# A planned mixer kernel: class statistics moved to ScalarE, the first tile in halves, and an order chosen among drawn ones

## The chip, the cores and the metric

The kernel runs on one core of a Trainium2 chip. The core has five engines that run at the same time and each take their own instructions in order: TensorE (PE: matrix products; PEld are its weight loads), VectorE (DVE), ScalarE (ACT), GpSimd (POOL) and SyncE (SP), which here issues transfers (DMA). The metric is the device time of one launch in microseconds (us), the median of several runs.

## What is computed

A sliding, dilated attention and a channel MLP, both on the same normalised input, multiplied and added to it (32 heads of 16, window 8, dilation 2, 2048 rows of 512, MLP width 1376):

```python
xn = _layernorm(x)
# A: q, k, v from xn @ wqkv; row s attends to rows s, s-2, ..., s-14
logits = einsum("bhsd,bhswd->bhsw", q, kg) * scale      # masked with -1e9 where s-2w < 0
attn = softmax(logits)
s = einsum("bhsw,bhswd->bhsd", attn, vg).reshape(B, S, D) @ wo
# B: normalised again, then Dense-GELU-Dense
y = _layernorm(xn)
g = silu(gelu(y @ w1 + b1) @ w2 + b2)
return x + s * g
```

## The kernel before

**Data.** Even and odd rows never meet in the attention, so there are two classes `c` of 1024 rows, each in eight tiles of 128 rows (`NI = 8`). Float32 values enter products as a high and a low float16 half, so that a product takes three matmuls (high·high, high·low, low·high); weights are scaled by powers of two found from their sums of squares.

**Start.** The tiles of class 0 are loaded and normalised in the order 2, 3, 0, 1, (4, 5), (6, 7) (`GROUPS`, `ln0`, L550). Per group: VectorE takes mean and variance (`stats`, L533); POOL works out the scaling (`factors`, L503: two small linear steps on the variance at L514 and L524, powers of −1/2 at L517 and L526, products at L521, L528 and L530); VectorE scales the tile (L571), or ScalarE for groups in `ACT_Y` (`y_act`, L538); TensorE transposes it (L578); ScalarE copies the result (L584, for tiles 2 and 3, which TensorE then multiplies in float32 at L651 while the weights are still being split) or casts it to its high half (L590), and VectorE takes the low half (L592). Until there is real work, TensorE runs `WAKE0` + `WAKE` idle matmuls (L1063).

**Weights.** `prep_q` (L469) finds the scale of a block of wqkv and splits it (L474, L492, L494). The MLP's w1 is squared and summed by ScalarE in four pieces (L392); the high halves of all four are written by VectorE (L443, `W1DVE`), the low halves too (L446). w2 follows (L445, L446).

**Units.** There are eight units `u`, a class and a block of eight heads each. `qkv` (L623) makes q, k and v of a unit in one of two buffers U (L644, ScalarE evicts at L661; halo copies by DMA at L670). `attention` (L689) then works on VectorE: four products q·k (L704), each summed over the 16 columns of a head (L707), maximum, difference (L727, L728), exponential on ScalarE (L730), sum, reciprocal, scaling (L732 to L734), four products with v (L760) that are added up (L755), a part of that by POOL "beside" VectorE (L783, L784), output halves (L743, L745) and a transposing DMA (L748). A buffer U is free for `qkv` of unit u + 2 once the unit's products have been taken.

**MLP.** `mlp1` (L905) multiplies one of 11 blocks of w1 with 512 rows (L914), Gelu at L931, high half at L935; the low half is made by VectorE (L939) where the step's number is in `DVE_LO`, else by a product on TensorE that subtracts the high half (L945) and ScalarE (L948). `mlp2` (L952, product at L961) follows two steps behind; Silu at L977. Results of the first product lie in two buffers `mh`.

**Class 1.** `ln1` (L597) loads each of the eight tiles, takes mean and variance by `stats` on VectorE, then `factors` for all eight, loads them again, scales them on ScalarE (L539), and makes the halves (L613, L614), which a transposing DMA brings into place (L616). **End.** `wo_first` and `wo_last` multiply with wo (L830), multiply with the MLP's result, and `finish` (L819) adds x: on VectorE for all tiles of class 0 (L821), on POOL for every second tile of class 1 (L823).

**Order.** Nothing is issued while the kernel is described: `Plan.add` notes each operation with its engine, a duration, what it reads and writes, and a priority. `Plan.issue` (L204) then places all of them on a modelled clock: per engine it takes, of those that could start soonest, the one with the lowest priority number, gives it buffers, and moves the clock; the instructions are then emitted in the order found. `port=True` marks VectorE and POOL operations that the model doesn't let overlap; ScalarE operations with a `table` that is not loaded cost 1.3 more. So a change of one constant can move any instruction.

Of the kernel before, what the change touches and what calls it, by code (L numbers as in the profile page):

```python
# [38 lines left out]
GROUPS = [(2,), (3,), (0,), (1,), (4, 5), (6, 7)]  # L39
# [4 lines left out]
ACT_Y = (1, 4, 5)  # L44

W1DVE = (0, 1, 2, 3)
# [7 lines left out]
DVE_LO = range(8, 44)  # L54
# [23 lines left out]
class Op:  # L78
    __slots__ = ("eng", "dur", "fn", "prio", "table", "bufs", "preds", "succs", "npred",
                 "ready", "nbytes", "n", "port", "rate", "issue", "tail", "slack")  # L80


class Plan:
# [9 lines left out]
    def add(self, eng, dur, fn, reads=(), writes=(), prio=None, table=None, nbytes=0,  # L93
            after=None, holds=(), port=False, rate=350e3, issue=0.55, tail=1.4, slack=0.0):
# [16 lines left out]
        o.port, o.rate, o.issue, o.tail, o.slack = port, rate, issue, tail, slack  # L111
        o.prio = self.prio if prio is None else prio
# [39 lines left out]
    def start(self):  # L152
        for o in self.ops:
            o.npred, o.ready, o.succs = len(o.preds), 0.0, []
        for o in self.ops:
            for p in o.preds:
                p.succs.append(o)
        self.free = {o.eng: 0.0 for o in self.ops}
        self.portfree, self.dma, self.landed, self.table = 0.0, 0.0, [], None

# [8 lines left out]
    def place(self, o, t):  # L169
# [15 lines left out]
        if o.eng == "act" and o.table is not None and o.table != self.table:  # L185
            end += 1.3
            self.table = o.table
        self.free[o.eng] = end
        if o.port:
            self.portfree = end  # L190
# [13 lines left out]
    def issue(self):  # L204
# [6 lines left out]
        while len(order) < len(self.ops):  # L211
            best = None
            for e, cand in engs.items():
                lst = []
                for o in cand:
                    t = self.earliest(o)
                    ok = True
# [18 lines left out]
            engs[o.eng].remove(o)  # L236
            for b in o.bufs:
                if b.slot is None:
                    r = b.ring.free
                    b.slot = r.index(min(r))  # L240
                    r[b.slot] = float("inf")
# [6 lines left out]
            for x in self.done(o, end, MARGIN):  # L248
                engs[x.eng].append(x)
            order.append((t, o))  # L250
        self.end = max(self.free.values())
        for t, o in order:
            o.fn()

# [16 lines left out]
WAKE0 = 26  # L271
# [28 lines left out]
def tile_mixer(ctx, tc, a_x, a_wqkv, a_wo, b_w1, b_b1, b_w2, out):  # L300
# [18 lines left out]
    def dve(n, fn, r, w, f=1.0, port=True, c=0.065, **k):  # L319
        pl.add("dve", c + n * DVE1 * f, fn, r, w, port=port, **k)  # L320

    def act(n, fn, r, w, aps=1, **k):
        pl.add("act", 0.07 + n * ACT1 + 0.093 * aps, fn, r, w, **k)
# [113 lines left out]
    def split(hi, lo, src, s, r, w, eng="act", n=None):  # L437
# [6 lines left out]
        else:  # L444
            act(n, lambda: nc.scalar.activation(hi, get(), AF.Identity, scale=s), r, [(w, "hi")])  # L445
        dve(n, lambda: nc.vector.scalar_tensor_tensor(lo, get(), s, hi, op0=ALU.mult,  # L446
                                                      op1=ALU.subtract), r + [(w, "hi")], [w], c=0.125)
# [21 lines left out]
    def prep_q(hb):  # L469
        col = R_s.new()  # L470
        for k in range(0, KT, 2):
# [5 lines left out]
            act(768, go, [("stq", hb, k)] + ([("yf", 2)] if hb == 0 else []), [(col, k), ("wqh", hb, k), ("wqh", hb, k + 1)],  # L477
# [8 lines left out]
        for k in range(0, KT, st):  # L486
# [9 lines left out]
                r + hk, [("wq", hb, j) for j in range(k, k + st)], holds=stkey[hb], c=0.125,  # L496
# [6 lines left out]
    def factors(n, mv, mk, cdst, ckeys, bias=True, pp=None):  # L503
# [6 lines left out]
        V = lambda: mv()[:, 0:n, 1]  # L510
        a0 = lambda: A.t[:, 0:n]
        a1 = lambda: A.t[:, 8:8 + n]
        small, power = 0.21, 0.42 + 0.14 * n
        pool(small, lambda: nc.gpsimd.tensor_scalar(  # L514
            p0b.t[:, 0:n], V(), (1.0 + EPS) / YS ** 2, EPS * EPS / YS ** 2, op0=ALU.mult, op1=ALU.add),
            mk, [p0b], prio=pp, port=False)
        pool(power, lambda: nc.gpsimd.tensor_tensor(  # L517
            rb.t[:, 0:n], p0b.t[:, 0:n], halves[:, 0:n], op=ALU.pow), [p0b], [(rb, 0)], prio=pp, port=False)
        if bias:
            for a in range(n):  # L520
                pool(small, lambda a=a: nc.gpsimd.tensor_scalar(  # L521
                    rb.t[:, 8 + a:9 + a], mv()[:, a:a + 1, 0], rb.t[:, a:a + 1], -1.0, op0=ALU.mult, op1=ALU.mult),
                    [mk[a], (rb, 0)], [(rb, 1, a)], prio=pp, port=False)
        pool(small, lambda: nc.gpsimd.tensor_scalar(  # L524
            a0(), V(), EPS, YS ** -2, op0=ALU.add, op1=ALU.mult), mk, [(A, 0)], port=False)
# [731 lines left out]
```

## Time and profile before

The page reports busy time per engine (an engine is busy while an instruction runs on it), the stretches in which it idled, and what ended a wait; "L661" is a line of the kernel, "ps<-wq,yT" its output and inputs.

| | |
|---|---|
| median of 3 runs | 422.49 us (421.89 to 422.58) |
| the profiled execution, its time | 421.77 us |
| the profiled execution, its span | 420.0 us |
| L914, L961: first and second MLP product, main forms | 456 and 480 matmuls of 512 columns, a group of 12 takes 2.59 us |
| L644: q, k, v | 744 matmuls of 384 columns, 12 take 1.95 us |
| L704, L707 on VectorE | 32 × 2290 ns, 32 × 2280 ns |
| L760, L755 on VectorE, 2048 columns | 28 × 2285 ns, 16 × 2282 ns |
| L535, L536: mean and variance | 16 × 0.68 us, 16 × 0.18 us |
| L784 on POOL | 21 × 2.35 us |
| L931, L935 on ScalarE, main forms | 38 × 749 ns, 38 × 684 ns |
| ScalarE table loads | 1283 ns each, 8 of them at L730 |

A group of matmuls advances TensorE by less than the sum of their durations, as they overlap. A busy share close to one on two engines says that either can hold the other; which of them does is read from the waits of each stage.

### The profile page before, as it was taken

Reading aid. Unit: us, or ns where it says so; the run is one execution under the profiler, and the core shown is the slowest. Engines: PE = TensorE matmul, PEld = TensorE weight load, DVE = VectorE, ACT = ScalarE, POOL = GpSimd, SP = SyncE. Lnnn points to the kernel's source line nnn. Section 1 sums busy time; section 2 is a strip of 40 time slices with the busy share of each in tenths; the row PEclk is TensorE's granted clock in tenths of the full one; section 3 lists DMA queues with packets and bytes.
Section 4 is the critical chain, followed back from the end, with each engine's and each line's share of the span. In section 5 each row is a group of like instructions: output and inputs, shape, how many; then the busy total and the mean of one; then the engine's idle time right before and its main releaser. Section 6 shows DMA issues by size and latency. Waiting matters only on the chain.

```text
span 420.0 us, 5549 instructions
## 1 busy us (share of the span) xinstructions
PE 410.1 (98%) x2107; PEld 209.5 (50%) x2107; DVE 387.7 (92%) x365; ACT 211.6 (50%) x314; POOL 91.8 (22%) x166
## 2 busy tenths in 40 slices
PE   7989999999999999999999999999999999999995
PEld 5556544445554465445544654454445544444442
DVE  4867999999999999899999999999999989999983
ACT  3899983953437842853358335334121393236400
POOL 7810200000463043002500430052002500250031
PEclk9999999999999999999999999999999999999999
DMA  8964440120025247611262022006423383007152
GB/s 298 413 234 140 126 163 0 61 91 0 2 87 126 77 108 163 154 39 26 87 151 100 2 87 52 1 20 193 150 85 123 88 209 111 2 0 204 52 144 102
DMA packets 42666, 44.83 MB, mean 107 GB/s; under 512 B 27496, under 2 KB 27936, under 8 KB 42128
## 3 DMA queue, kind: packets, MB, share of 16 engines
q1 hardware_dynamic: 42640, 44.49, 35.0%
q8 instruction: 16, 0.26, 0.3%
q14 instruction: 10, 0.08, 0.1%
HBM read 23.53 MB, written 7.34 MB: 74 GB/s over the span
## 4 chain that ended last, share of the span: by engine, by line
PE 78%; DVE 10%; POOL 3%; issue 3%; DMA 2%; ACT 1%; SPq 0%; DVEq 0%; POOLq 0%; ACTq 0%
PE ps L644 22%; PE z L961 22%; PE mh L914 21%; PE ps L830 6%; PE z L830 2%; DVE prod L704 2%; PE mh L644 2%; DVE prod L760 2%; DVE L L707 2%; PE mh L830 1%; PE ps L914 1%; DMA U<-U 1%; DVE f L614 1%; POOL lw L517 1%; DMA f<-in_A_x_dram 1%
## 5 line engine op out<-in xcount | busy, mean ns | idle before, releaser
L914 PE MATMUL mh<-yT,w 128*128 128x512 f16 (+1 forms) x504 | 115.5, 379 | 0.1
L644 PE MATMUL ps<-wq,yT 128*128 128x384 f16 x684 | 114.5, 326 | 0.9 <-ACT U L661 0.8
L961 PE MATMUL z<-w,h 128*128 128x512 f16 x480 | 111.4, 379 | 0.6 <-ACT f L977 0.6
L644 PEld LDWEIGHTS <-yT 128*128 128x128 f16 x744 | 72.7, 98 | 49.5 <-issue 1.1
L914 PEld LDWEIGHTS <-w 128*128 128x128 f16 (+1 forms) x528 | 52.8, 100 | 61.3 <-issue 0.4
L961 PEld LDWEIGHTS <-h 128*128 128x128 f16 x480 | 47.0, 98 | 56.0 <-issue 1.1
L704 DVE TENSOR_TENSOR prod<-U 128x2048 f32<-128x2048 f32 x32 | 73.1, 2290 | 1.6 <-DMA U<-U 0.6
L707 DVE TENSOR_REDUCE L<-prod 128x128 f32<-128x2048 f32 x32 | 72.8, 2280 | 0.4
L931 ACT ACTIVATE mh<-mh,b1T,hsc 128x512 f32<-128x512 f32 (+1 forms) x42 | 31.4, 749 | 81.5 <-PE mh L914 81.4
L760 DVE TENSOR_TENSOR prod<-L,U 128x2048 f32<-128x2048 f32 x28 | 63.5, 2285 | 0.3
L661 ACT ACTIVATE U<-ps,cs 128x384 f32<-128x384 f32 x58 | 33.0, 578 | 56.1 <-PE ps L644 50.0
L783 POOL COPY gate<-prod 1x1 f32<-1x1 f32 x21 | 4.4, 208 | 238.3 <-DVE prod L704 235.0
L755 DVE TENSOR_TENSOR prod<-prod,prod 128x2048 f32<-128x2048 f32 x16 | 36.5, 2282 | 0.0
L784 POOL TENSOR_TENSOR prod<-prod 128x1024 f32<-128x1024 f32 x14 | 32.9, 2349 | 0.0
L830 PEld LDWEIGHTS <-oT 128*128 128x128 f16 x189 | 18.5, 98 | 22.1
L830 PE MATMUL ps<-wo,oT 128*128 128x512 f16 x120 | 27.2, 379 | 0.0
L935 ACT ACTIVATE h<-mh,hsc 128x512 f16<-128x512 f32 x38 | 26.0, 684 | 0.8
L939 DVE SCALAR_TENSOR_TENSOR h<-mh,hsc,h 128x512 f16<-128x512 f32 x32 | 23.9, 746 | 2.1 <-ACT h L935 2.0
L743 ACT ACTIVATE o<-prod,osc 128x1024 f16<-128x1024 f32 (+1 forms) x9 | 9.5, 1054 | 29.9 <-POOL prod L784 23.9
L784 POOL TENSOR_TENSOR prod<-prod,prod 128x1024 f32<-128x1024 f32 x7 | 16.4, 2347 | 0.0
L931 ACT ACT_TABLE_LOAD x11 | 14.1, 1283 | 0.2
L823 POOL TENSOR_TENSOR U<-U,f 128x512 f32<-128x512 f32 x4 | 5.1, 1268 | 33.5 <-DVE U L893 33.5
(161 smaller groups left out, 366.8 us busy)
## 6 DMA issues: line engine op xcount, KB each, us to landing
f<-in_A_x_dram SPq DMA_DIRECT2D x31, 256.0 KB, 4.3
U<-U SPq DMA_DIRECT2D x16, 392.0 KB, 4.0
gd<-f SPq DMA_DIRECT2D x12, 256.0 KB, 2.1
oT<-in_B_w_dram SPq DMA_DIRECT2D x2, 1024.0 KB, 10.0
yT<-in_B_w_dram SPq DMA_DIRECT2D x2, 1024.0 KB
f<-gd SPq DMA_DIRECT2D x8, 256.0 KB, 2.9
out_dram<-f SPq DMA_DIRECT2D x8, 256.0 KB, 2.6
out_dram<-U SPq DMA_DIRECT2D x7, 256.0 KB, 2.2
```

Of the source, the lines that this page charges most:

```text
L644: nc.tensor.matmul(b.t[:, 0:384], y[:, s, k, o:o + P], wq[:, hb, t, k], start=(n == 0), stop=(n == 11))
L661: act(384, lambda i=i, b=b: nc.scalar.activation(U3[:, i:i + 31:15, :], b.t[:, 0:384].rearrange("p (t e) -> p t e", t=3), AF.Identity, sca ...
L704: dve(2048, lambda p2=p2, g=g: nc.vector.tensor_tensor(p2(), q, slots(Ut, KH, 2 * g), op=ALU.mult), qk + [("kh", ub, 0), ("kh", ub, 1), (" ...
L707: dve(2048, lambda pr=pr, g=g: nc.vector.tensor_reduce(L3()[:, 2 * g:2 * g + 2], pr.t.rearrange("p (r f d) -> p r f d", r=2, d=DH), AX.X, ...
L755: dve(n, lambda: nc.vector.tensor_tensor(d(), a(), b(), op=ALU.add), keys, [dkey])
L760: dve(2048, lambda: nc.vector.tensor_tensor(pr.t.rearrange("p (r f d) -> p r f d", r=2, d=DH), L3()[:, 2 * g:2 * g + 2].rearrange("p r (f ...
L784: nc.gpsimd.tensor_tensor(x.t[:, 0:1024], x.t[:, 0:1024], y(), op=ALU.add)
L830: nc.tensor.matmul(b.t, oT[:, hb, i // 4, s, i % 4], wo[:, t, hb], start=(hb == 0 and n == 0), stop=(hb == last and n == 2))
L914: nc.tensor.matmul(b.t[0:M], w1[:, s, k, f * P:f * P + M], yT[ch][:, t, k], start=(n == 0), stop=(n == 11))
L931: act(512, lambda: nc.scalar.activation(b.t[0:M], b.t[0:M], AF.Gelu_apprx_tanh, bias=b1T[0:M, f:f + 1], scale=hsc[0:M, 1:2]), [b, ("b1T",) ...
L935: act(512, lambda: nc.scalar.activation(hi()[0:M], b.t[0:M], AF.Identity, scale=hsc[0:M, 2:3]), [b] + [("hseq", NF * ch + f - 1)] * (NF * ...
L961: nc.tensor.matmul(z.t, hl[s][0:K, t * P:(t + 1) * P], w2[0:K, w, f], start=(f == 0 and n == 0), stop=(f == NF - 1 and n == 2))
```

## The change

- **Class 1's statistics on ScalarE.** In `ln1` the two VectorE instructions per tile give way to three ScalarE ones: a pass that sums the tile, a one-column step that turns the sum into a scaled negative mean, and a pass of squares around it that sums to the variance. The small linear steps of `factors` become VectorE instructions in both classes; for class 0 they are fused behind the statistics of each tile, and the power is taken tile by tile. In class 1 the products at the end of `factors` move to VectorE too.
- **First tile in halves.** Tile 2 is scaled, transposed and copied in two halves of 256 columns (`in_halves`); its float32 products wait for the half that they read.
- **A product next to its sums.** An operation can name a successor (`then`) that the planner places directly behind it: each q·k product and its reduction.
- **The exponential's table.** A one-column exponential is placed once the last reduction of a unit is there, and until the real one is placed no operation with another table may go to ScalarE (`hold`).
- **Order.** `issue` draws an order for each of four seeds, with durations disturbed at random, replays each order under eight other disturbances, and takes the one with the lowest mean end; that order is then drawn again undisturbed.
- **Constants.** Groups 0 and 1 become one; ScalarE scales tile 4 alone; ScalarE takes the high halves of w1's second and fourth piece; steps 8 and 9 of the MLP make their low half by TensorE and ScalarE; half of class 0's tiles get x added on POOL; four more idle matmuls; modelled durations change by a few hundredths of a microsecond; a second load of a class-1 tile waits for the tile three back and not two back.

```diff
-GROUPS = [(2,), (3,), (0,), (1,), (4, 5), (6, 7)]
+GROUPS = [(2,), (3,), (0, 1), (4, 5), (6, 7)]
...
+HALVED = 2
+
+ACT_Y = (4,)
+
+W1DVE = (0, 2)
...
-DVE_LO = range(8, 44)
+DVE_LO = range(10, 44)
...
+        if o.hold is not None:
+            self.held = o.hold
...
-                    ok = True
+                    ok = not (self.held and o.table is not None and o.table != self.table)
...
+                o = o.then if o.then in engs[o.eng] and all(b.slot is not None for b in o.then.bufs) else None
...
+    def judge(self, seed, times=8):
...
+        self.draw(seed, 0.7)
+        order = self.order()
+        t = 0.0
+        for n in range(times):
+            self.draw(-1 - n)
+            t += self.replay(order) / times
+        return t, order
+
+    def issue(self):
+        self.lengths = [(o.dur, o.tail, o.rate) for o in self.ops]
+        best = min(SEEDS, key=lambda seed: self.judge(seed)[0]) if len(SEEDS) > 1 else SEEDS[0]
+        order = self.judge(best, 0)[1]
+        self.draw(0)
         for t, o in order:
             o.fn()
...
+SEEDS = (100, 486, 604, 1142)
...
-WAKE0 = 26
+WAKE0 = 30
...
-        pool(small, lambda: nc.gpsimd.tensor_scalar(
-            p0b.t[:, 0:n], V(), (1.0 + EPS) / YS ** 2, EPS * EPS / YS ** 2, op0=ALU.mult, op1=ALU.add),
-            mk, [p0b], prio=pp, port=False)
...
+        def operand(a, m):
+            dve(m, lambda: nc.vector.tensor_scalar(
+                p0b.t[:, a:a + m], V(a, m), (1.0 + EPS) / YS ** 2, EPS * EPS / YS ** 2, op0=ALU.mult, op1=ALU.add),
+                mk[a:a + m], [(p0b, j) for j in range(a, a + m)], port=False)
+            if a + m == n:
+                dve(n, lambda: nc.vector.tensor_scalar(
+                    a0(), V(0, n), EPS, YS ** -2, op0=ALU.add, op1=ALU.mult), mk, [(A, 0)], port=False)
...
+    def in_halves(i, x, xkey, mv, mk, rb, a, first, way):
+
+        y, yf = R_f.new(), R_L.new()
+        yF[i] = yf
+        for h in range(2):
+            c = slice(h * 256, h * 256 + 256)
+            dve(256, lambda c=c: nc.vector.tensor_scalar(
+                y.t[:, c], x()[:, c], mv()[:, a, 0:1], rb.t[:, a:a + 1], op0=ALU.subtract, op1=ALU.mult),
+                [xkey, (rb, 0, a), mk], [(y, h)] + [("yd", i)] * h, f=0.72, c=0.12, **first)
+            b = R_z[1 + (i + 2 * h) % 3].new()
...
+            pe(2, P, tr, [(y, h)], [b], fp32=2, **first)
+            act(256, lambda b=b, c=c: nc.scalar.copy(yf.t[:, c], b.t[:, 0:256]), [b], [(yf, h)] + [("yf", i)] * h,
+                aps=0, **way)
...
-            stats(lambda: mv1, i, mk[i], lambda x=x: x.t, [x])
-        rb = factors(NI, lambda: mv1, mk, cT[:, 1, :], [("c", 1, i) for i in range(NI)])
+
+            m = R_cs.new()
+            act(760, lambda x=x, i=i: nc.scalar.activation(x.t, x.t, AF.Identity, accum_out=mv1[:, i, 0:1]),
+                [x], [x, (m, 0)])
+            act(1, lambda m=m, i=i: nc.scalar.activation(m.t[:, 0:1], mv1[:, i, 0:1], AF.Identity, scale=-(D ** -1.5)),
+                [(m, 0)], [m])
+            act(760, lambda x=x, i=i, m=m: nc.scalar.activation(
+                x.t, x.t, AF.Square, bias=m.t[:, 0:1], scale=D ** -0.5, accum_out=mv1[:, i, 1:2]), [x, m], [x, mk[i]], aps=2)
+        rb = factors(NI, lambda: mv1, mk, cT[:, 1, :], [("c", 1, i) for i in range(NI)], [True] * NI)
...
-            dve(2048, lambda pr=pr, g=g: nc.vector.tensor_reduce(
+
+            first.then = dve(2048, lambda pr=pr, g=g: nc.vector.tensor_reduce(
...
+        act(1, lambda: nc.scalar.activation(warm, ident[0:1, 0:1], AF.Exp), [(L, 3)], [("warm",)],
+            table="exp", prio=PEV, hold=True)
...
-        act(512, lambda: nc.scalar.activation(L.t, L.t, AF.Exp, scale=DH ** -0.5), Lk, Lk, aps=0,
-            table="exp", prio=PEV)
+        act(512, lambda: nc.scalar.activation(L.t, L.t, AF.Exp, scale=DH ** -0.5), Lk + [("warm",)], Lk, aps=0,
+            table="exp", prio=PEV, hold=False)
...
-            finish(0, i, lambda g=g: g.t, [g, x], lambda x=x: x.t)
+            finish(0, i, lambda g=g: g.t, [g, x], lambda x=x: x.t, "pool" if i % 2 else "dve")
```

199 lines of the change are left out of this document (128 added, 71 removed).

## The prediction

> **What bounds the kernel now.** I read the busy times first, then the busy share of each engine by stage, then who waited for whom on TensorE, then the first eight microseconds in order of time. All times are microseconds.
>
> ```profile
> span 420.0 us, 5549 instructions
> PE 410.1 (98%) x2107; PEld 209.5 (50%) x2107; DVE 387.7 (92%) x365; ACT 211.6 (50%) x314; POOL 91.8 (22%) x166
> PEclk9999999999999999999999999999999999999999
> ```
>
> TensorE is busy for all but 9.9 of 420.0, at full clock throughout. The stages show where the 9.9 lie (second number: length; then busy time of PE, PEld, DVE, ACT, POOL):
>
> ```profile
> 0.00:5.00 5.00, 3.96 (x24) 2.92 (x24) 1.05 (x4) 1.28 (x1) 3.69 (x14) 1.00 0.64 193
> 5.00:10.00 5.00, 3.89 (x25) 2.85 (x24) 3.10 (x7) 2.67 (x6) 4.00 (x14) 1.00 1.03 387
> 15.00:20.00 5.00, 4.64 (x31) 2.76 (x28) 3.67 (x9) 4.11 (x8) 4.46 (x12) 1.00 1.04 412
> 20.00:25.00 5.00, 3.85 (x27) 2.48 (x26) 3.13 (x9) 4.61 (x10) 2.80 (x6) 1.00 1.00 395
> 40.00:50.00 10.00, 10.00 (x60) 5.63 (x59) 9.30 (x24) 9.90 (x19) 2.53 (x1) 1.00 0.28 81
> 100.00:120.00 20.00, 20.00 (x121) 11.95 (x120) 20.00 (x20) 7.29 (x11) 7.46 (x12) 1.00 0.15 46
> 190.00:230.00 40.00, 39.42 (x207) 20.50 (x207) 39.38 (x27) 20.43 (x28) 7.88 (x12) 1.00 0.31 90
> 410.00:420.00 10.00, 5.30 (x28) 2.47 (x26) 3.74 (x7) 0.00 (x0) 1.27 (x1) 1.00 0.29 105
> ```
>
> Idle TensorE: 1.04 before its first instruction, 1.11 in 5 to 10, 1.51 in 15 to 25, 4.70 behind its last matmul, and only 1.55 in all the rest (0.58 in 130 to 150, 0.27 in 150 to 190, 0.58 in 190 to 230, 0.12 in 310 to 350). VectorE is full as well, from about 50 on: it is the second bound, less than a microsecond per stage behind the first. So a cut in VectorE's or ScalarE's work pays only through these gaps and through an earlier start; what can be had is some four microseconds, and one new wait inside 25 to 415 costs its whole length.
>
> The start, in order of time:
>
> ```profile
> 3.37 0.69 DVE L535 BATCH_NORM_STATS2 bn<-prod 128x6 f32<-128x512 f32 x1 [2.37 <-DMA prod<-in_A_x_dram]
> 4.10 0.18 DVE L536 BATCH_NORM_AGGREGATE lw<-bn 128x2 f32<-128x6 f32 x1
> 4.46 0.19 POOL L514 TENSOR_SCALAR lw<-lw 128x1 f32<-128x1 f32 x1 [0.51 <-DVE lw L536]
> 4.74 0.19 POOL L524 TENSOR_SCALAR lw<-lw 128x1 f32<-128x1 f32 x1
> 5.01 0.56 POOL L517 TENSOR_TENSOR lw<-lw,halves 128x1 f32<-128x1 f32 x1
> 5.61 0.55 DVE L571 TENSOR_SCALAR f<-prod,lw,lw 128x512 f32<-128x512 f32 x1 [1.33 <-POOL lw L517]
> 6.21 0.66 PE L578 MATMUL z<-ident,f 128*128 128x128 f32 x4 [1.08 <-DVE f L571]
> 6.91 0.58 ACT L584 COPY L<-z 128x512 f32<-128x512 f32 x1 [4.90 <-PE z L578]
> 7.54 0.91 PE L651 MATMUL ps<-prod,L 128*128 128x384 f32 x2
> ```
>
> One tile goes through five engines before the first useful product at 7.54; what TensorE does until then (L1063) is idle work that counts as busy.
>
> **The change, part by part.**
>
> *Start (normalisation of class 0, first tile in halves).* The two small POOL steps at 4.46 and 4.74 become VectorE instructions fused behind the aggregate. A one-column VectorE instruction takes 0.15 and follows its neighbour by 0.19 (L411 to L418, 24.51 to 24.70), so the operand is there at 4.28 + 0.19 = 4.47, the power starts after the hand-over of 0.18 (4.28 to 4.46) at 4.65 and not at 5.01, and ends at 5.22. The first half of the scaling, 256 columns, is bounded by half of 0.55 and all of it; I take 0.36, which leaves 0.19 fixed. It ends at 5.61. Transposes begin at 5.66; four plus hand-over took 0.70 (6.21 to 6.91), two less at 0.165 make 0.37: 6.03. A ScalarE column costs 0.75 ns (0.83 for 768 columns at L474, 0.64 for 512 at L1125), so the copy of 256 is 0.58 less 0.19 = 0.39: 6.42. First product at 6.47, **1.1 earlier** (bounds: 0.4 with only the power's share, 1.3 with halves at half price). The second half is copied by 6.81 and needed after the first two products, 1.56 later: hidden. The other class-0 tiles gain on POOL the same two steps each; POOL was 4.46 of 5 busy in 15 to 20, its scaling terms sat ahead of the next tile's power. Tiles 0 and 1 become one group, and tiles 1 and 5 are scaled by VectorE (0.55) where ScalarE took 0.81. So the tiles that TensorE waited for in 15 to 25 come earlier. Of that 1.51 I take **1.2** (bounds: 0, if another engine keeps them; 1.5, all). Price on VectorE: 13 small instructions and two scalings, 13 × 0.19 + 2 × 0.55 = 3.6, in 5 to 25, where it idles 5.3 of 20.
>
> *Second class's mean and variance.* Out of VectorE: eight statistics at 0.68 and eight aggregates at 0.18, **6.9**, half of them in 30 to 50. Five small instructions of eight columns come back, 5 × 0.19 = 1.0. Into ScalarE: per tile a sum, a one-column multiply and a square with sum; the nearest rows are 0.64 plus 0.21 for the read-out (L1125), 0.20 (L1155), and 0.81 plus 0.21 (two pointer operands, L539): 2.1, times eight 16.6 on an engine at 50%. SP's eight loads of these tiles now wait for ScalarE instead of VectorE, and the halo copies (L670) queue behind them on SP; that wait costs SP 0.3 now and I keep 0.3.
>
> *VectorE elsewhere.* High halves of two w1 pieces go to ScalarE: 1.24 + 0.41 = 1.65 off VectorE, about 2.4 onto ScalarE, less the two scalings of 0.81 that left it. Two low halves of the first MLP chunk (f = 8, 9) leave VectorE, 2 × 0.75, and return as one TensorE matmul and one ScalarE step each. A matmul of 512 columns advances TensorE by 2.59 / 12 = 0.216, so **+0.43** on the bound, certain. Four of the eight finishing adds of class 0 go to POOL: 4 × 0.68 off, 4 × 1.27 on POOL (L823). After 57 VectorE is thus lighter by 3.4 + 1.5 + 2.7 − 1.0 = 6.6, in 30 to 57 by 3.4 + 1.65 = 5.1. That is the cover for running TensorE earlier: it has to stay ahead by as much as TensorE gains, which is under four.
>
> By the Trainium skill (SBUF — State Buffer, "SBUF: two separate sides") a GpSimd instruction and a VectorE instruction with two SBUF inputs hold the shared ports against each other for a whole instruction. This trace agrees in the last stretch: the adds of L821 take 0.68 alone, 0.90 on average beside L823. By the rule the four adds cost VectorE up to 5.1 where I count a relief of 2.7.
>
> *Order.* Each q·k product is followed at once by its reduction; a table load for the exponential is put ahead, and no Gelu may go between it and the exponential; eight noisy replays choose among four drawn orders. None of it adds work but eight one-column ScalarE steps (0.20 each, ScalarE idles half the time). What it does to waits is bounded by the 1.55 of idle time in 25 to 415 on one side and by the third rival on the other. The waits there are for late VectorE and ScalarE results (0.85 at 190.58 for an eviction that waited for L760), which the lighter VectorE helps. I take **1.0** of the 1.55. The four more idle matmuls at the start lie ahead of the first transposes: 4 × 0.107 in a gap of 1.08.
>
> *Sum.* −1.1 − 1.2 − 1.0 + 0.43 = −2.9 on a span of 420.0. The profiled execution took 421.77, 1.8 around its span; the three runs have a median of 422.49, 0.7 above it. −2.9 from the median is **419.6**. With all gaps and 1.3 at the start it is 418.6; with half of the three gains, 421.3.
>
> **The rivals.**
> 1. *ScalarE gives the start back.* It is 9.90 of 10 busy in 40 to 50, and the first MLP (47.04) needs w1 and w2 split. With 0.8 more work net there, TensorE's earlier arrival would end in a wait before the MLP. Against it: VectorE's w1 chain gets 1.65 shorter, and the piece of w1 that is ready last, at 47.43, is read only by the tenth matmul of the first MLP step, at 47.20 + 9 × 0.216 = 49.1. Time: 422.49 − 1.0 + 0.43 = 421.9.
> 2. *The replays change little and the early gaps stay*: only the first tile counts, −1.1 + 0.43: 421.8.
> 3. *The hold and the pairs delay the MLP (slower).* Its place is ScalarE beside each softmax, seen in the third unit:
>
> ```profile
> 163.79 0.69 DVE L727 TENSOR_REDUCE mx<-L 128x64 f32<-128x512 f32 x1
> 166.46 0.75 ACT L931 ACTIVATE mh<-mh,b1T,hsc 128x512 f32<-128x512 f32 x1 [1.57 <-PE mh L914]
> 169.31 1.28 ACT L730 ACT_TABLE_LOAD   x1
> 170.60 0.63 ACT L730 ACTIVATE L<-L 128x512 f32<-128x512 f32 x1
> ```
>
> The Gelu at 166.46 went ahead of the exponential; held, it goes behind. A result of L914 must be through Gelu, high half and low half within 7.8 (two buffers, steps of 5.18, less 2.59); these take 0.75 + 0.69 + 0.75 and hand-overs, 2.3. Add a hold of 2.2 at best (0.69 + 0.69 + 0.63), Gelu's own reload 1.28, and on VectorE a product with its reduction ahead of the low half, 4.6: 10.4, which is 2.6 too long. Half of that in four of seven units is +5.2; with the gains above, 424.8. It decides once a held Gelu meets such a pair. For it: in six of eight units a Gelu now lies between the maximum (L727) and the exponential. Against: the load no longer stands behind the difference, which brings the exponential 1.28 forward, and a Gelu in just that place leaves TensorE only 0.27 idle in 150 to 190. The Trainium skill (ScalarE: Activation LUTs, "What ACT_TABLE_LOAD costs") puts a switch at 2.66 with its drain; the rows show 1.28 and the exponential 0.01 behind it. By its figure the overrun would be 4.0 and the time, by the same half in four units, about 427.6.
> 4. *POOL's adds hold VectorE up.* At the price of 4 × 1.27 lost instead of 2.7 gained, VectorE after 57 is lighter by 6.6 − 2.7 − 5.1 = −1.2, so no lighter; its last output (L745 ends at 403.3; TensorE reads it, through a transposing transfer, from 404.93 + 9 × 0.216 = 406.9 on) then holds the end where it was: 422.0.
>
> **How the numbers follow.** Forecast 0.62; rival 1 0.09; rival 2 0.08; rival 3 0.15; rival 4 0.04; 0.02 for anything else. A measurement of this kernel tells 0.2%, 0.84, from no change, so faster means under 421.65: the forecast, and a third of rivals 1 and 2 at their lower ends: 0.67. Same, to 423.33: 0.16; slower: 0.17. The forecast's own range is 418.6 to 421.3. The range for 8 in 10 is 417.6 to 423.4: it holds rivals 1, 2 and 4, leaves out most of rival 3 above, and goes 1.0 under the forecast's own range, for the spread of the runs (0.7) and short waits that I did not count.
>
> **What would show it.** The first L651 product near 6.47, not 7.54; TensorE's idle time in 15 to 25 near 0.3; VectorE's busy time down to about 380, ScalarE's up to about 230; sixteen more one-column ScalarE instructions (eight for the tables, eight for the means), two more L945-type matmuls; idle time in 25 to 415 near 0.5. The forecast is wrong if TensorE idles over 2 in 25 to 415: at the first MLP step (rival 1), or at L914 behind a held Gelu (rival 3).

## The result and the profile after

| | before | after |
|---|---|---|
| median | 422.19 us (421.6 to 422.58, 4 runs) | 418.1 us (417.75 to 418.42, 4 runs) |
| span of the profiled execution | 420.0 us | 416.0 us |

The ratio is 0.9904, with a 95% interval of 0.9887 to 0.9921: the change makes the kernel 4.1 us faster, where 2.9 was forecast.

The time lies inside the range for 8 in 10 (417.6 to 423.4), but 0.5 under the forecast's own range (418.6 to 421.3).

The winning order is not, as the description of the change has it, drawn again undisturbed. The second argument of `judge(best, 0)` is the number of replays; the same disturbed order is drawn again and issued.

The head of the page after, busy time per engine:

```profile
span 416.0 us, 5582 instructions
...
PE 409.4 (98%) x2113; PEld 210.4 (51%) x2113; DVE 380.9 (92%) x362; ACT 228.0 (55%) x366; POOL 94.2 (23%) x142
```

VectorE's 387.7 became 380.9 and ScalarE's 211.6 became 228.0, near the 380 and 230 that were said. TensorE's busy time hardly moved; its idle time did, from 9.9 to 6.6. Where, is in the stages (length, then busy time of PE, PEld, DVE, ACT, POOL):

```profile
5.00:10.00 5.00, 4.61 (x25) 2.83 (x23) 3.80 (x15) 2.50 (x7) 3.65 (x11) 1.00 1.04 371
...
15.00:20.00 5.00, 5.00 (x38) 3.60 (x36) 4.93 (x12) 5.00 (x10) 2.73 (x5) 1.00 1.05 414
20.00:25.00 5.00, 5.00 (x37) 3.58 (x36) 4.16 (x14) 4.84 (x10) 2.41 (x5) 1.00 0.99 393
...
60.00:80.00 20.00, 19.22 (x94) 9.12 (x93) 19.48 (x27) 17.88 (x34) 0.17 (x2) 1.00 0.24 80
...
130.00:400.00 270.00, 270.00 (x1372) 134.83 (x1370) 255.53 (x185) 120.70 (x173) 56.30 (x76) 1.00 0.33 89
```

The last of these stretches in the kernel before:

```profile
130.00:400.00 270.00, 268.45 (x1355) 133.27 (x1353) 262.46 (x191) 124.94 (x172) 48.23 (x72) 1.00 0.34 92
```

From 15 to 25 the 1.51 of idle time are gone, and from 130 to 400 there is none left (the kernel before has 1.55 there). One new gap is in 60 to 80: 0.78. In the late stretch VectorE idles 14.5 of 270 where it idled 7.5, so it is no longer the second bound at once behind the first. The start, in order of time:

```profile
3.34 0.69 DVE L632 BATCH_NORM_STATS2 bn<-prod 128x6 f32<-128x512 f32 x1 [2.33 <-DMA prod<-in_A_x_dram]
...
4.36 0.14 DVE L599 TENSOR_SCALAR lw<-lw 128x1 f32<-128x1 f32 x1
4.59 0.56 POOL L608 TENSOR_TENSOR lw<-lw,halves 128x1 f32<-128x1 f32 x1 [0.63 <-DVE lw L599]
5.20 0.74 DVE L700 TENSOR_SCALAR f<-prod,lw,lw 128x256 f32<-128x256 f32 x2 [0.70 <-POOL lw L608]
5.67 0.44 PE L708 MATMUL z<-ident,f 128*128 128x128 f32 x2 [0.32 <-DVE f L700]
6.14 0.77 ACT L710 COPY L<-z 128x256 f32<-128x256 f32 x2 [0.80 <-PE z L708]
6.56 2.20 PE L776 MATMUL ps<-prod,L 128*128 128x384 f32 x6
```

The chain is the forecast's, step by step and within a tenth: power at 4.59 (4.65 was said), the first half of the tile scaled by 5.6, the first float32 product at 6.56 (6.47). Not all of the closed gap is work, though. TensorE's idle matmuls are placed by the planner, and ten of the 34 now lie behind the first product:

```profile
13.00 0.38 PE L1191 MATMUL z<-fours 128*128 128x256 bf16 x2
...
14.31 0.38 PE L1191 MATMUL z<-fours 128*128 128x256 bf16 x2
...
17.35 0.82 PE L1191 MATMUL z<-fours 128*128 128x256 bf16 x6
```

They take 1.09 in all and count as busy. So a gap is better counted between starts of real matmuls than by the busy share. Counted so, the 4.0 us of the spans come from:

| stretch | forecast | measured |
|---|---|---|
| first float32 product | −1.1 | −0.98 (7.54 to 6.56) |
| from there to 25 | −1.2 | −1.71: 1.67 of waits behind q, k, v products gone, 1.13 of float32, summing and transposing steps and the waits among them gone, idle matmuls +1.09 |
| 25 to the last matmul, waits | −1.0 | −1.45: old ones of 2.39 gone, a new one of 0.94 |
| two more matmuls that subtract | +0.43 | +0.43 |
| behind the last matmul | 0 | −0.33 (4.70 to 4.37) |
| sum | −2.9 | −4.0 |

The 2.39 is more than the 1.55 of idle time in the same stretch, because the end of the matmul ahead lies inside a wait: idle time shows the wait shorter than the distance between starts does (0.94 by starts is 0.78 as idle time).

### The profile page after: what moved, and what is told of

Same layout as the page of the kernel before. It is cut to its first block, busy times and chain, and to the rows that moved or that the text cites. A ratio compares the mean times of both kernels' runs of the same rounds, so it can differ in the third digit from the quotient of the medians.

```text
span 416.0 us, 5582 instructions
## 1 busy us (share of the span) xinstructions
PE 409.4 (98%) x2113; PEld 210.4 (51%) x2113; DVE 380.9 (92%) x362; ACT 228.0 (55%) x366; POOL 94.2 (23%) x142
## 4 chain that ended last, share of the span: by engine, by line
PE 97%; DMA 1%; DVE 1%; ACT 0%; issue 0%; POOL 0%; DVEq 0%
PE z L1089 27%; PE ps L769 27%; PE mh L1042 26%; PE ps L958 6%; PE mh L769 2%; PE z L958 2%; PE mh L958 1%; PE ps L1042 1%; PE z L675 1%; PE ps L776 1%; PE mh L776 1%; DMA prod<-in_A_x_dram 1%; PE mh L1073 0%; PE z L1191 0%; PE ps L478 0%
## 5 line engine op out<-in xcount | busy, mean ns | idle before, releaser
L912 POOL TENSOR_TENSOR prod<-prod 128x1024 f32<-128x1024 f32 x14 | 32.9, 2348 | 0.0
L1067 DVE SCALAR_TENSOR_TENSOR h<-mh,hsc,h 128x512 f16<-128x512 f32 x30 | 22.3, 744 | 2.7 <-ACT h L1063 2.6
L873 DVE SCALAR_TENSOR_TENSOR o<-prod,osc,o 128x1024 f16<-128x1024 f32 (+1 forms) x9 | 10.5, 1166 | 7.7 <-ACT o L871 7.7
L912 POOL TENSOR_TENSOR prod<-prod,prod 128x1024 f32<-128x1024 f32 x7 | 16.5, 2350 | 0.0
L951 POOL TENSOR_TENSOR f<-f,f 128x512 f32<-128x512 f32 x4 | 9.0, 2260 | 23.0 <-DVE f L972 20.6
```

The source lines that it names most:

```text
L912: nc.gpsimd.tensor_tensor(x.t[:, 0:1024], x.t[:, 0:1024], y(), op=ALU.add)
```

## The experiments

Each kernel's time is a median; the kernel before, run beside them, had 421.98, 422.09 and 422.06 us in the three sets (experiments 1 to 4, 5 to 8, 9 to 12), and ratios are to it. The kernel after was not run again with them, so differences from its 418.1 are between sets. Where an edit changes the work, the order has to be drawn anew: the seed is then the best of 300 by the kernel's own replays. So a difference between two kernels can in part be the draw: from experiment 1 to after it is 0.2, but experiment 2, which has the work of before in another order, takes 1.9 longer than before. Theory: the gain is supply at the start and a lighter VectorE later. Rivals: it is the choice of the order; it is the statistics alone; the hold costs. A time "at" which TensorE waits is the start of the last matmul ahead of the wait; the wait is counted by starts.

**1. The order from undisturbed durations.** All work of the change, no choice among draws.

```diff
-SEEDS = (100, 486, 604, 1142)
+SEEDS = (0,)
```

> All of the change, but the order is the one that the planner draws from undisturbed durations; no choice among drawn orders. If the gain comes from the lighter VectorE, the halves and the earlier tiles (the prediction's sum), this order has the same start (first float32 product near 6.5 us) and at most 1 us more idle TensorE in 25 to 410 us: 418.1 to 419.5 us. Rival, that the choice of the order carries most of it: several waits of TensorE between 25 and 410 us, together 3 us or more, and 421 us or more, no better than the kernel before.

418.31 us (417.92 to 418.4), ratio 0.991 (0.9895 to 0.9924). First product at 7.14 and not near 6.5 (the first statistics start 0.26 later than in after, and TensorE is at its slower rate until 7.07, see the last section), and the same single wait of 0.94 at 77.7. The choice among drawn orders is worth 0.2 here, which these runs can't tell from nothing.

**2. The work of before in a drawn order.** The planner of after with its durations around the kernel before.

```diff
+def judge(self, seed, times=8):
...
-pl.add("act", 0.07 +
+pl.add("act", 0.11 +
...
-    small, power = 0.21, 0.42 + 0.14 * n
+    small, power = 0.28, 0.46 + (0.16 if n < 3 else 0.4) * n
```

> The kernel before with nothing of its work changed; only the planner is the new one (durations as the change has them, one order drawn from disturbed durations, the best of 300 by replays). If the lighter VectorE and the halves carry the gain, this stays within 1 us of the kernel before (421.2 to 423.2 us): the first float32 product stays near 7.5 us and the idle time in 15 to 25 us stays over 1 us. If the choice of the order carries it, the idle time in 25 to 410 us falls from 1.55 us to under 0.5 us and the time to 420.5 us or less.

423.87 us, ratio 1.0044 (1.0029 to 1.0059): slower, and 0.7 above the range expected. TensorE waits 1.53 at 14.5 (for a tile that ScalarE scales), 0.99 and 0.47 at 17.9 and 19.0, 1.08 and 0.92 at 142.6 and 146.2, and its tail is 6.02. Together with the first: no order by itself brought the gain, so the work is what has changed. The new work in the order of the old planner was not tried.

**3. Class 1's statistics back on VectorE.**

```diff
-            act(760, lambda x=x, i=i: nc.scalar.activation(x.t, x.t, AF.Identity, accum_out=mv1[:, i, 0:1]),
...
+            stats(lambda: mv1, i, mk[i], lambda x=x: x.t, [x])
```

> All of the change, but the second class's mean and variance are taken by VectorE again (order drawn anew, the best of 300 by replays). If VectorE's 6 us are what covers the earlier TensorE: 1 to 2.5 us slower than the change (419 to 420.6 us), with idle TensorE in 100 to 400 us where q, k and v wait for a buffer that VectorE still reads. Rival, that TensorE alone bounds the kernel and VectorE has cover to spare: within 0.4 us of the change (418.1 us), and the wait of 0.78 us at 78 us, which ScalarE's queue makes, is gone.

419.04 us (418.78 to 419.38), ratio 0.9929 (0.9914 to 0.9944); VectorE busy 385.6, ScalarE 214.1. TensorE's waits behind the start (total, times, longest):

```profile
PE mh L1036 <- ACT h L1070: 0.8, 1, 0.8
PE ps L763 <- ACT yT L690: 0.5, 1, 0.5
```

The first is the wait of after (0.94 by starts, at 78.35). The second is new: at 24.7, behind the last idle matmuls, TensorE waits 0.70 by starts for the high half of a class-0 tile. Neither is for VectorE, and the tail is 4.37 as in after. Counted from the first statistics, the last matmul ends 0.85 later, nearly all of it this new wait and one more idle matmul behind the first product (11 where after has 10). So the time lies in the range that was expected, but not for the reason given: no wait for VectorE came back in 100 to 400, and the statistics alone were not what kept VectorE ahead.

**4. The first tile whole.**

```diff
-HALVED = 2
+HALVED = -1
```

> All of the change, but the first tile is scaled, transposed and copied whole (order drawn anew, the best of 300 by replays). By the prediction's working the halves carry 0.7 us of the 1.1 us at the start, the shorter chain of small steps 0.4 us: first float32 product near 7.2 us and a time of 418.8 us. Rival, that the weights or the second tile are late in any case: the first product at 7.2 us but the first float16 product of q, k and v no later than in the change (13.7 us), and the time within 0.2 us of 418.1 us.

418.14 us (418.0 to 419.18), ratio 0.9906 (0.989 to 0.9923). The first product comes 3.79 after the first statistics instruction; in after it is 3.22, in before 4.17. So the halves bring it 0.57 earlier (0.7 was said), and the first q, k, v starts at 14.32, 0.66 later than in after. Yet the time is the same: the rival's time, though not with its sign, as the first q, k, v does come later. The profiled execution is the 419.18 one, with a wait of 0.84 at 168; without that its last matmul, counted from the first statistics, is 0.35 late. What the halves are worth lies under what the drawn orders differ by.

**5. No early table load.** The one-column exponential and the hold are taken out.

```diff
-        act(1, lambda: nc.scalar.activation(warm, ident[0:1, 0:1], AF.Exp), [(L, 3)], [("warm",)],
-            table="exp", prio=PEV, hold=True)
...
-            table="exp", prio=PEV, hold=False)
+            table="exp", prio=PEV)
```

> All of the change, but without the one-column exponential that loads the table early, and so without the stretch in which no Gelu may go to ScalarE (order drawn anew, the best of 300 by replays). In the change, the plain-order run and the runs with statistics on VectorE and a whole first tile, TensorE waits 0.78 us near 77 us for a result that went behind the held exponential. If the hold makes that wait (the prediction's third rival, on a small scale): the wait is gone and 1 us with it, 416.9 to 417.4 us. Rival, that it is ScalarE's length of queue there, with the weights' split ahead, and not the hold: the wait stays, 418.0 us; and if the early load shortened VectorE's softmax enough to matter, waits of VectorE for the exponential grow and the time goes to 419 us.

417.05 us (416.86 to 417.78), ratio 0.9877 (0.9861 to 0.9894), 1.05 under after. The intervals of the two ratios overlap from 0.9887 to 0.9894; what bears it out is that TensorE waits nowhere from 25 to 405. The profiled execution is the slowest of the four (417.78): its last matmul ends at 411.60 as in after, because its first q, k, v starts at 14.71, 1.05 later than there, and the wait that is gone makes up for that. To see why the wait is gone, first the stretch around the new wait in the kernel after, in order of time:

```profile
66.57 2.75 PE L1042 MATMUL mh<-yT,w 128*128 128x512 f16 x12
67.55 1.28 ACT L853 ACT_TABLE_LOAD   x1
68.84 0.20 ACT L853 ACTIVATE warm<-ident 1x1 f32<-1x1 f32 x1
...
71.81 0.62 ACT L858 ACTIVATE L<-L 128x512 f32<-128x512 f32 x1
72.45 1.28 ACT L1059 ACT_TABLE_LOAD   x1
73.74 0.75 ACT L1059 ACTIVATE mh<-mh,b1T,hsc 128x512 f32<-128x512 f32 x1
...
75.43 0.68 ACT L1063 ACTIVATE h<-mh,hsc 128x512 f16<-128x512 f32 x1
...
77.14 0.38 PE L1073 MATMUL mh<-h,dg 128*128 128x512 f16 x1
77.56 0.69 ACT L1076 ACTIVATE h<-mh,hsc 128x512 f16<-128x512 f32 x1 [0.62 <-PE mh L1073]
78.30 2.75 PE L1042 MATMUL mh<-yT,w 128*128 128x512 f16 x12 [0.78 <-ACT h L1076]
```

The product at 66.57 has its result at 69.3, but the table was taken for the exponential at 67.55, so Gelu waits until 73.74, behind the exponential and a load of its own table. High half, subtracting matmul and low half follow, and only then is a buffer `mh` free for the product at 78.30. The same place without the hold:

```profile
70.52 0.75 ACT L1057 ACTIVATE mh<-mh,b1T,hsc 128x512 f32<-128x512 f32 x1 [0.31 <-PE mh L1040]
71.29 1.28 ACT L856 ACT_TABLE_LOAD   x1
72.59 0.63 ACT L856 ACTIVATE L<-L 128x512 f32<-128x512 f32 x1
72.91 2.75 PE L1040 MATMUL mh<-yT,w 128*128 128x512 f16 x12
```

Gelu goes ahead at 70.52, the exponential is 0.8 later, and TensorE's next product starts at 72.91 with no wait. Of the nine kernels with the hold seven show the same wait of 0.94 near 78 (after and 1, 3, 4, 6, 8, 10; 7 and 9 don't); of the five without it (before and 2, 5, 11, 12) none does. The third rival's mechanism is real. It met TensorE once and cost 0.94 there, where the rival had 1.3 in each of four units.

**6. The change's own order without the ten late idle matmuls.**

```diff
+        idle = [o for t, o in order if o.prio == 1e9][24:]
         for t, o in order:
-            o.fn()
+            if o not in idle:
+                o.fn()
```

> The change's own order, instruction for instruction, without the ten idle matmuls that this order puts behind the first float32 product (the first 24 stay). If they hold up TensorE (they take 1.09 us between 12.7 and 18.2 us in the change's trace, 0.11 us each): up to 1.1 us faster, 417.0 to 417.5 us, and the first MLP matmul near 39.2 us instead of 40.2 us. Rival, that TensorE had to wait there in any case for transposed tiles and split weights: the same stretches turn up as idle time, 418.1 us within 0.2 us.

417.69 us (417.19 to 417.96), ratio 0.9892 (0.9878 to 0.9907): 0.4 less than after, of the 1.09 that was taken out, with runs that overlap by 0.2; it lies between the two times that were expected. Waits at q, k, v of 0.23, 0.15 and 0.15 took their place, so half of that time was a true gap. And in this execution the first 24 idle matmuls ran longer:

```profile
1.05 5.30 PE L1193 MATMUL z<-fours 128*128 128x256 bf16 x24 [1.05 <-DVE s L1248]
6.14 0.64 PE L710 MATMUL z<-ident,f 128*128 128x128 f32 x2
```

In after the same 24 take 4.29. The first half of the tile was there at 5.69, so here the idle matmuls themselves held the first transposes back by 0.45.

**7. The supply of class 0 as before.** Small steps on POOL, tiles 0 and 1 apart, ScalarE scales tiles 1, 4 and 5; the rest is the change (the power is still taken tile by tile).

```diff
-GROUPS = [(2,), (3,), (0, 1), (4, 5), (6, 7)]
+GROUPS = [(2,), (3,), (0,), (1,), (4, 5), (6, 7)]
...
-ACT_Y = (4,)
+ACT_Y = (1, 4, 5)
...
-            dve(m, lambda: nc.vector.tensor_scalar(
+            lin(m, lambda: v.tensor_scalar(
```

> All of the change, but class 0 is normalised as before: the small linear steps on POOL, groups (0) and (1) apart, tiles 1, 4 and 5 scaled by ScalarE (order drawn anew, the best of 300 by replays). If the faster supply of tiles carries the 1.5 us of idle time that the change removed in 15 to 25 us: idle time or idle matmuls of 1 us or more come back between 13 and 25 us, the first float32 product goes from 6.56 to 6.9 us, and the time is 419.3 to 420 us. Rival, that a new order alone closes these gaps: under 0.4 us idle there, and 418.1 to 418.6 us.

420.37 us (419.74 to 421.27), ratio 0.996 (0.9948 to 0.9973): 2.3 slower than after. The stages of the start (columns as above):

```profile
5.00:10.00 5.00, 4.31 (x18) 2.19 (x16) 2.56 (x7) 2.06 (x6) 2.75 (x8) 1.00 0.99 354
10.00:15.00 5.00, 4.24 (x23) 2.64 (x22) 4.83 (x15) 3.68 (x7) 4.32 (x11) 1.00 1.02 425
15.00:20.00 5.00, 4.78 (x33) 3.34 (x32) 4.37 (x10) 4.31 (x9) 4.24 (x13) 1.00 1.04 409
20.00:25.00 5.00, 4.61 (x32) 2.88 (x30) 4.00 (x7) 4.20 (x9) 4.92 (x14) 1.00 1.01 402
```

TensorE idles 2.06 from 5 to 25 (after: 0.39), and from 10 on POOL is 4.2 to 4.9 of 5 busy (after: 2.4 to 4.0). VectorE scales a tile at 21.17 after it has idled 0.72 for POOL's power; in before it was 0.88, at 21.39, for the tile that TensorE waited longest for. The profiled execution is the slowest of the six (421.27): its last matmul ends 2.5 later than in after, and the tail is 5.26 (after: 4.37). Groups, small steps and scaling were undone together, so no run tells them apart.

**8. Steps 8 and 9 of the MLP make their low half on VectorE again.**

```diff
-DVE_LO = range(10, 44)
+DVE_LO = range(8, 44)
```

> All of the change, but steps 8 and 9 of the MLP take their low half on VectorE again, as before (order drawn anew, the best of 300 by replays). Two matmuls less on TensorE: 0.43 us less, 417.7 us, if VectorE has cover for two more instructions of 0.75 us, as the run with the statistics on VectorE says. Rival, that VectorE is late in 80 to 110 us: a new wait of TensorE for VectorE there and 418.5 us or more.

417.51 us (417.07 to 418.42), ratio 0.9892 (0.9876 to 0.9908): 0.6 faster by the medians, with the ranges overlapping. Counted from the first statistics, the last matmul ends 0.46 earlier; 0.11 of that is one idle matmul less behind the first product, so 0.35 is left for the two matmuls, which are priced at 0.43. This part of the change was not needed.

**9. All the VectorE work of before.** Statistics, w1's high halves, the two low halves and the finishing adds go back together.

```diff
-W1DVE = (0, 2)
+W1DVE = (0, 1, 2, 3)
...
-DVE_LO = range(10, 44)
+DVE_LO = range(8, 44)
...
-lambda x=x: x.t, "pool" if i % 2 else "dve")
+lambda x=x: x.t)
...
+            stats(lambda: mv1, i, mk[i], lambda x=x: x.t, [x])
```

> All of the change's start, pairs, early table and planner, but VectorE's work behind the start is as before: the second class's statistics, four high halves of w1, the low halves of steps 8 and 9, and all finishing adds of class 0 on VectorE, some 12 us more than in the change (order drawn anew, the best of 300 by replays). If the lighter VectorE is what took the three waits of 25 to 410 us away: waits of 2 us or more come back there and the time is 420 us or more, though TensorE has 0.43 us less to do. Rival, that TensorE alone bounds the kernel here too (putting back the statistics alone brought no wait): no new wait and 417.5 to 418.5 us.

422.11 us (421.54 to 422.47, 10 runs), ratio 0.9996 (0.9987 to 1.0006): the whole gain is gone, though the new start, the pairs and the planner are all in it. Who waited for whom on TensorE (total, times, longest):

```profile
PE mh L1036 <- DVE h L1061: 1.1, 1, 1.1
...
PE z L952 <- DMA oT<-o: 0.6, 1, 0.6
PE z L1083 <- ACT f L1099: 0.5, 2, 0.3
PE ps L952 <- DMA oT<-o: 0.4, 1, 0.4
```

and its last 5 us:

```profile
415.00:420.00 5.00, 0.00 (x0) 0.00 (x0) 2.22 (x5) 0.00 (x0) 1.61 (x1) 0.63 0.61 220
```

TensorE waits for a low half by VectorE (1.25 by starts at 131.1), twice, as in before, for a result of ScalarE in the second MLP product (0.36 and 0.51, near 128) and, twice, for the transposed attention output that VectorE delivers last (390.4 and 410.4). Behind the last matmul 6.18 pass where after has 4.37. VectorE's busy time is 393.1: 12 more than after, and 5.4 more than before, as the small steps and two scalings of the new supply stay on it. So this is the old work and the new supply's price on VectorE together.

**10. No product placed next to its sums.**

```diff
-            first.then = dve(2048,
+            dve(2048,
```

> All of the change, but a product of q and k and its reduction need not be neighbours (order drawn anew, the best of 300 by replays). If the pairs carry something: POOL's additions again meet products on VectorE, single VectorE instructions of 0.5 us and more beyond their own duration, and 418.8 us or more. Rival, that they do not matter as VectorE has cover: 417.9 to 418.4 us.

419.55 us (418.96 to 419.82), ratio 0.9939 (0.9925 to 0.9954), 1.4 slower. VectorE's instructions are stretched by 3.8 in all (those by over 0.2 beyond the median of their kind), the largest here:

```profile
153.89 2.34 POOL L912 TENSOR_TENSOR prod<-prod,prod 128x1024 f32<-128x1024 f32 x1
153.92 2.86 DVE L738 TENSOR_TENSOR f<-f,f 128x512 f16<-128x512 f32 x1 [0.24 <-ACT f L737]
```

A VectorE step of 0.69 took 2.86: POOL's started 0.03 ahead of it and ended at 156.23, and it ended 0.55 behind that. The next largest is 1.07 at 304.27, in one of VectorE's long additions. In after these stretches sum to 1.0. Then, at 167.3, TensorE waits 1.10 for a low half by VectorE. But pairs are not what keeps such steps apart in general: the kernels of before, 2 and 12 have none, and their stretches sum to 0.6, 0.3 and 0.3. And experiment 4, with the pairs, shows a wait of 0.84 for the same kind of low half at 168. So whether the 1.4 is the missing pairs or this draw stays open.

**11. The parts that paid.** The change without hold and early table, with low halves 8 and 9 on VectorE and with 20 idle matmuls.

```diff
-DVE_LO = range(10, 44)
+DVE_LO = range(8, 44)
...
-            table="exp", prio=PEV, hold=False)
+            table="exp", prio=PEV)
...
+        idle = [o for t, o in order if o.prio == 1e9][20:]
```

> The change without the early table and its hold, with the low halves of steps 8 and 9 on VectorE as before, and with 20 idle matmuls, all of them ahead of the first tile. If the three effects found so far add up (1.0 for the hold's wait, 0.4 to 0.6 for the two matmuls and their ScalarE steps, 0.4 for the idle matmuls): 416.0 to 416.3 us. Rival, that they share one cause near 77 us or that a new order makes another wait: 416.9 us or more.

416.46 us (416.18 to 416.49), ratio to before 0.9866 (0.985 to 0.9882), 1.6 under after with runs that don't overlap (416.46 / 418.1 = 0.996, by medians of different sets). It beats both kernels, and misses the sum that was expected by 0.2. Its page:

```profile
PE 408.6 (99%) x2097; PEld 209.3 (50%) x2097; DVE 383.6 (93%) x364; ACT 226.5 (55%) x356; POOL 95.4 (23%) x142
```

TensorE has 0.8 less work than in after, and waits nowhere from 25 to 405.

**12. The new supply alone.** The work of before and the planner of after, as in 2, with the change's groups and small steps for class 0. Class 1's small steps and last products on VectorE, its later second loads and the four more idle matmuls are in it too.

```diff
-GROUPS = [(2,), (3,), (0,), (1,), (4, 5), (6, 7)]
+GROUPS = [(2,), (3,), (0, 1), (4, 5), (6, 7)]
...
+            dve(m, lambda: nc.vector.tensor_scalar(
+                p0b.t[:, a:a + m], V(a, m), (1.0 + EPS) / YS ** 2, EPS * EPS / YS ** 2, op0=ALU.mult, op1=ALU.add),
```

> The work of the kernel before, with one part of the change alone: class 0's small linear steps on VectorE, groups (0) and (1) joined, only tile 4 scaled by ScalarE (new planner, the best of 300 orders by replays). It stands against the run of the kernel before with the new planner, 423.9 us. If the supply of tiles is the largest term by itself (2.3 us when it was taken out): 421 to 422 us, with under 0.5 us idle in 13 to 25 us. Rival, that it pays only where VectorE is relieved behind it, as its small steps and two scalings load VectorE with 3.6 us: 423 us or more, with the waits moved behind 25 us.

420.64 us (420.41 to 421.15), ratio 0.9969 (0.9956 to 0.9982), 3.2 under experiment 2 and 1.4 under before (422.06); as experiment 2 has waits of its own at 142.6 and 146.2, the smaller figure is the safer one. It is faster than the 421 to 422 expected. Its last matmul ends at 411.66, as in after (411.60), with one wait of 0.48 for a low half by VectorE at 128.8. But the tail is 7.25 where after has 4.37. The stretches at its end:

```profile
400.00:412.00 12.00, 11.66 (x57) 5.39 (x55) 9.03 (x12) 0.72 (x1) 2.92 (x2) 1.00 0.36 93
412.00:419.00 7.00, 0.00 (x0) 0.00 (x0) 3.82 (x8) 0.00 (x0) 2.91 (x2) 0.77 0.59 215
```

and of after:

```profile
400.00:412.00 12.00, 11.60 (x57) 5.38 (x55) 7.95 (x12) 0.00 (x0) 5.87 (x4) 1.00 0.46 150
412.00:416.00 4.00, 0.00 (x0) 0.00 (x0) 1.18 (x4) 0.00 (x0) 0.00 (x0) 0.72 0.39 139
```

VectorE's last attention output starts at 404.30, in after at 399.81 (before: 402.56). TensorE does other products first while it waits for that output, so the finishing adds bunch up behind the last matmul: 3.82 of VectorE and 2.91 of POOL, where after has 1.18 and none.

## Why the forecast held, step by step

**The start (−1.1; 0.98 measured).** The chain was right link by link. What was mis-credited is what it is worth: the halves account for 0.57 of the earlier product, but a kernel without them (experiment 4) takes the same time. That points to the tiles behind the first one as what TensorE is short of, more than its first product. And the four more idle matmuls did not stay ahead of the first transposes, as the forecast had it: ten lie behind the first product.

**The gaps to 25 (−1.2; 1.71 measured).** The mechanism was right: POOL's queue of small steps held the tiles back. The size was too small. Undoing groups, small steps and scaling costs 2.3 (experiment 7, some 0.9 of it a longer tail), where the forecast had 1.2 here and 0.4 for the shorter chain of the first tile; adding them alone brings 1.4 (12). And 1.09 of the closed gap is idle matmuls; about half of that time could be had (experiment 6).

**The waits later on (−1.0; 1.45 measured).** "The lighter VectorE helps" was right, for VectorE's relief as a whole: with its old work back, low-half and output waits and the long tail return (experiment 9). The size was too small because the forecast went by idle time, 1.55, where the waits are 2.39 by starts. The choice of the order, to which the forecast gave no price of its own, brought nothing that could be measured (1), and a new order for the old work brought a loss (2). For the pairs the forecast had no price either; the kernel without them is 1.4 slower (10), which may be its draw. These prices don't add up: undoing supply costs 2.3, VectorE's relief 4.0 and the pairs 1.4, together 7.7 of a gain of 4.1. Without its relief, and in the draw without the pairs, VectorE is late, which is one limit and not two; the supply has gaps of its own before 25, and a longer tail besides. Moving the statistics alone (3) or the low halves alone (8) uncovers none. The other two parts, w1's high halves and the finishing adds, weren't tried alone, so how the 4.0 is shared out stays open.

**The two matmuls (+0.43).** Exact, and not needed (8). The forecast counted their VectorE relief as cover; there was cover enough without it.

**The tail (0; −0.33).** The forecast held it fixed at 4.70. It is not: it runs from 4.25 to 7.25 among these kernels, and is long where VectorE's last output is late (2, 9, 12). This is one way by which a lighter VectorE pays even when TensorE's last matmul doesn't move.

**The rivals.** The first, ScalarE giving the start back, didn't happen: ScalarE is 9.97 of 10 busy in 40 to 50 and TensorE doesn't wait there. The second is refuted by the closed gaps; the replays do change little (1), but the gaps closed all the same. The third happened at one place, at 77, for 0.94; the forecast's "a Gelu in just that place leaves TensorE only 0.27 idle" was too mild for one that also needs the subtracting matmul, and the rival's four units too many. On its table load, the Trainium skill (ScalarE: Activation LUTs, "What ACT_TABLE_LOAD costs") has 2.66 us with the drain; here the load takes 1.28 and the next instruction starts 0.01 behind it (67.55, 68.84), so the trace doesn't agree on the drain. The fourth was wrong about who pays. One of the four adds on POOL, and a VectorE add beside another step of POOL (L912, 321.27 to 323.62):

```profile
317.94 3.25 POOL L951 TENSOR_TENSOR f<-f,f 128x512 f32<-128x512 f32 x1 [0.44 <-DVE f L972]
...
323.07 1.10 DVE L949 TENSOR_TENSOR f<-f,f 128x512 f32<-128x512 f32 x1
```

POOL's took 2.26 on average where such an add took 1.27 before. By the four adds VectorE was held 0.37, at 330.9, where the rival charged 5.1; the 0.40 at 323.07 is L912's, which the kernel before has as well. That either side may be the one that waits is what the Trainium skill says (SBUF — State Buffer, "SBUF: two separate sides": whichever starts first has the ports for its whole instruction). The trace agrees: at 317.94 VectorE's product had started 0.16 ahead of POOL's add, and at 330.9 POOL's add was 0.77 ahead of VectorE's step. Experiment 10's 2.86 agrees too. No instruction of TensorE waited behind POOL's longer adds.

## What to carry to other kernels

When two engines are full, look at when the second one delivers and not at its busy time alone: here its lateness came back as waits, or as a longer tail behind the last matmul. Undoing parts one at a time measures how far each uncovers the common limit, so such prices must not be added; where each part needs its order drawn anew, several draws per kernel would be needed to tell part from draw; a part that can be undone for nothing should be (here the hold, two subtracting matmuls and some idle ones, together 1.6). Work that only fills gaps, like idle matmuls, hides gaps from the busy share: count from one real start to the next.

## What had not been expected of the hardware

The time at which TensorE's clock becomes full differs from run to run. The first idle matmul starts at 1.04 or 1.05 in all of them; from start to start each takes 0.213 until the clock is full and 0.109 after. By the clock record of each trace that point was 3.72 in before, 4.15 in after, and 4.26 to 7.07 in the experiments. The Trainium skill (TensorE: Matmul & The Clock Gate, Part 1) explains such a spread by a window of about 3.4 us that runs freely; here it came 2.7 to 6.0 after the first matmul, and no run shows the window itself. Where it comes late, a fixed number of idle matmuls ends late as well: 24 of them lasted until 6.35 in experiment 6 and until 5.34 in after, and in the former they held real work back by 0.45.
